# A fused attention and SwiGLU kernel on one core: gamma loads moved behind the first k and v, two casts moved off VectorE, the turns of A's x interleaved with Z's columns, three later jobs changed

## The chip, the cores and the metric

The kernel runs on one core of one Trainium2 chip. The metric is device time in microseconds (us). Most executions agree within 0.3%, so an effect of a few tenths of a microsecond needs several timed runs. Only fast runs are compared.

Names: PE is the tensor engine, DVE is VectorE, ACT is ScalarE, POOL is GpSimd, SP is SyncE, the engine whose queue issues nearly all DMAs here. "Span" is the time from the first to the last instruction in the profile. The device time is longer than the span by about 2 us.

## The reference, cut to what matters

```python
# q, k, v: (8, 8, 576, 64) f32; d_model 512, d_ff 1536; 4608 tokens
kv  = einsum('bhsd,bhse->bhde', k, v)
out = einsum('bhsd,bhde->bhse', q, kv)
out = out / sqrt(mean(out*out, -1) + 1e-6) * g_norm
x   = out.transpose(0, 2, 1, 3).reshape(4608, 512)
xn  = x / sqrt(mean(x*x, -1) + 1e-6) * rms_g
g   = xn @ w_gate
y   = (g * sigmoid(g) * (xn @ w_val)) @ w_out      # (4608, 512) f32
```

## The kernel before

The kernel works in bf16. It has a prologue for batch 0 (0 to about 22 us), a middle part in which the FFN of batch 0 runs beside the attention of batch 1 (to about 62 us), and a loop in which the FFN of batch n hides the attention of batch n+1. The tokens of batch 0 are split in two halves, A and Z. Each half goes through the same chain: q columns, squares, sums, square root, scale, turn of x (a transposition), first FFN units. The first FFN units also need the first two blocks of w_gate and w_val, loaded as f32 and cast.

The loads at the start, in order of issue, are nearly all on SP's queue; only two v loads and the two small gamma loads are on ACT's:

```python
for j in (0, 1):
    load_kv(0, "k", nc.sync, slice(j, j + 1))
    load_kv(0, "v", nc.scalar, slice(j, j + 1))
SC.preload_act_table(ACT.Sqrt)
nc.scalar.dma_start(out=gam[0:NS, :], in_=moe_rms_g...)        # gamma, two small loads
nc.scalar.dma_start(out=gam[NS : NS + 1, :]..., in_=g_norm...)
load_q0(0, nc.sync)                                            # two DMAs
for j in (2, 3):
    load_kv(0, "k", nc.sync, slice(j, j + 1))
    load_kv(0, "v", nc.sync, slice(j, j + 1))
load_q0(1, nc.sync)                                            # two DMAs
for blk in range(2):
    for name in ("g", "v"):
        load_w(blk, name, nc.sync)                             # w_gate and w_val, blocks 0 and 1
```

Each DMA completes into one of eight semaphores that are taken in turn. An issue therefore waits until the DMA eight places earlier has landed. I call these the eight completion slots.

Near the end of the prologue, Z's square root and the casts of weight block 1:

```python
Z.head()
Z.root_by_table(lambda: round_w(1, "g", 2, DVE))   # the square root, on ACT
round_w(1, "g", 0, SC)                             # casts of w_gate block 1, ACT
round_w(1, "g", 3, SC)
round_w(1, "g", 1, GP)
xs = [Z.scale(c, oZ[c]) for c in range(2)]
...
```

In the loop, the normalised rows of the next batch are turned by DMA, four times, on SP's queue, and the next FFN waits for the fourth:

```python
def x_rows(self, c):
    ...
    nc.sync.dma_start_transpose(
        out=xnts[self.n][:, :, 128 * c : 128 * c + 128],
        in_=self.xna[c].rearrange("p h d -> p (h d)"),
    )
```

## Time and profile before

| | before |
|---|---|
| time, median of the first three runs | 324.34 us (324.08 to 324.5) |
| profiled run: time, span | 324.46, 322.7 us |
| PE busy | 316.0 us, 98% |
| PE waits listed | four groups, 2.3 us together, all before 21.6 us |
| second half of q of batch 0: last byte landed | 12.88 us |
| v of batch 1: last byte landed | 37.11 us |
| first down-projection matmul | 41.31 us |

All waits of PE of more than 0.15 us (engine, tile and line, what it waited for, total us, times, longest):

```profile
PE att_ps L617 <- DVE sel L606: 1.2, 1, 1.2
PE att_ps L640 <- DVE qb L108: 0.5, 2, 0.3
PE v_ps L489 <- DVE wv_sb L203: 0.4, 1, 0.4
PE g_ps L403 <- ACT qt L106: 0.2, 1, 0.2
```

Stretches of the kernel before (window, its length, busy us of PE, PEld, DVE, ACT and POOL, PE clock, DMA share, and last the GB/s that DMA moved):

```profile
10.00:12.00 2.00, 1.87 (x35) 0.85 (x28) 1.48 (x7) 0.99 (x3) 0.00 (x0) 1.00 1.03 331
12.00:14.00 2.00, 1.75 (x26) 1.11 (x25) 0.94 (x5) 0.38 (x1) 0.86 (x1) 1.00 1.09 362
```

### The profile page before, as it was taken

How to read it: one execution, taken by the hardware profiler on the slowest of the kernel's cores; microseconds unless marked ns; L12 is line 12 of the kernel's file. 1: busy time of each engine (PE TensorE's matmuls, PEld its weight loads, DVE VectorE, ACT ScalarE, POOL GpSimd, SP SyncE). 2: the span in 40 equal slices, each digit the busy share in tenths (PEclk: the TensorE clock that was granted, in tenths of full speed). 3: DMA queues.
4: the chain of work that ended last, by engine and by line, in shares of the span. 5: the costliest groups of instructions: out<-in, count | busy, mean ns of one | idle time of the engine just before them, and what ended most of it. 6: DMA issues, size and time to landing. Idle time of an engine off the chain costs nothing.

```text
span 322.7 us, 5143 instructions
## 1 busy us (share of the span) xinstructions
PE 316.0 (98%) x1925; PEld 156.5 (49%) x1925; DVE 181.5 (56%) x373; ACT 178.3 (55%) x318; POOL 20.3 (6%) x42
## 2 busy tenths in 40 slices
PE   8899999999999999999999999999999999999995
PEld 3575456554455445544554454445544444444443
DVE  4785767568438922793279417850696068703310
ACT  3576447666757475747664766576554355223321
POOL 1363251100000000000000000000000000000000
PEclk9999999999999999999999999999999999999999
DMA  7999999887379557924792378936102600240014
GB/s 277 355 351 386 377 374 293 214 265 176 65 195 295 132 143 163 328 54 114 187 328 56 73 202 222 315 55 169 43 2 49 182 31 1 48 147 4 0 35 98
DMA packets 74421, 54.87 MB, mean 170 GB/s; under 512 B 42264, under 2 KB 67100, under 8 KB 74396
## 3 DMA queue, kind: packets, MB, share of 16 engines
q1 hardware_dynamic: 74016, 53.88, 58.4%
q10 hardware_dynamic: 380, 0.66, 0.6%
q8 instruction: 15, 0.25, 0.3%
q14 instruction: 10, 0.08, 0.1%
HBM read 37.75 MB, written 9.44 MB: 146 GB/s over the span
## 4 chain that ended last, share of the span: by engine, by line
PE 92%; DMA 4%; DVE 2%; SPq 0%; ACT 0%; issue 0%; DVEq 0%
PE g_ps L472 28%; PE v_ps L472 28%; PE o_ps L516 27%; DMA st<-in_q_dram 3%; PE att_ps L272 2%; PE att_ps L343 2%; PE v_ps L516 1%; PE g_ps L516 1%; DVE xna L453 1%; DMA out_dram<-o_sb 1%; PE v_ps L489 1%; PE o_ps L489 1%; PE g_ps L489 0%; PE att_ps L338 0%; PE att_ps L285 0%; PE att_ps L265 0%
## 5 line engine op out<-in xcount | busy, mean ns | idle before, releaser
L478 DVE TENSOR_TENSOR h_sb<-silu,v_ps 128x512 bf16<-128x512 bf16 x104 | 71.0, 683 | 110.3 <-ACT silu L477 66.9
L472 PE MATMUL g_ps<-xnt,wg_sb 128*128 128x512 bf16 x416 | 106.8, 379 | 0.0
L472 PE MATMUL v_ps<-xnt,wv_sb 128*128 128x512 bf16 x416 | 106.7, 379 | 0.0
L477 ACT ACTIVATE silu<-g_ps 128x512 bf16<-128x512 f32 x104 | 62.5, 601 | 64.4 <-PE g_ps L472 53.7
L516 PE MATMUL o_ps<-wo_sb,h_sb 128*128 128x512 bf16 x396 | 87.4, 379 | 0.0
L472 PEld LDWEIGHTS <-wv_sb 128*128 128x128 bf16 x416 | 40.7, 98 | 49.1
L516 PEld LDWEIGHTS <-h_sb 128*128 128x128 bf16 x420 | 40.7, 98 | 47.7
L472 PEld LDWEIGHTS <-wg_sb 128*128 128x128 bf16 x416 | 38.7, 98 | 40.0 <-issue 0.4
L106 ACT COPY o_sb<-o_ps 128x512 f32<-128x512 f32 (+1 forms) x34 | 19.7, 580 | 38.0 <-PE o_ps L516 37.3
L361 DVE TENSOR_REDUCE ssq<-sq 128x16 f32<-128x1024 bf16 x28 | 34.1, 1219 | 1.0
L352 ACT ACTIVATE sq<-att_ps 128x512 bf16<-128x512 f32 x28 | 16.7, 597 | 13.1 <-PE att_ps L343 8.7
L106 ACT CAST vb<-st 128x512 bf16<-128x512 f32 (+2 forms) x33 | 18.9, 625 | 4.7 <-DMA st<-in_v_dram 4.7
L378 DVE TENSOR_TENSOR xna<-outa,s1y 128x512 bf16<-128x512 bf16 x28 | 17.9, 684 | 0.0
L354 ACT CAST outa<-att_ps 128x512 bf16<-128x512 f32 x28 | 16.2, 579 | 0.0
L106 ACT CAST qb<-st 128x1024 bf16<-128x1024 f32 (+1 forms) x15 | 14.2, 987 | 1.9 <-DMA st<-in_q_dram 1.9
L106 ACT CAST kb<-st 128x512 bf16<-128x512 f32 (+1 forms) x25 | 14.0, 619 | 0.0
L360 DVE TENSOR_TENSOR sq<-sq,gsq 128x512 bf16<-128x512 bf16 x28 | 11.7, 418 | 0.0
L343 PEld LDWEIGHTS <-qt 128*128 128x128 bf16 x96 | 7.4, 98 | 5.7
L343 PE MATMUL att_ps<-kv_all,qt 128*128 128x128 bf16 x96 | 9.3, 219 | 0.0
L272 PEld LDWEIGHTS <-kb 128*128 128x128 bf16 x120 | 7.7, 98 | 2.8
L617 PE MATMUL att_ps<-kv_all 128*128 128x512 bf16 (+1 forms) x21 | 7.6, 490 | 1.2 <-DVE sel L606 1.2
L272 PE MATMUL att_ps<-vb,kb 128*128 128x128 bf16 x120 | 8.7, 219 | 0.0
(141 smaller groups left out, 166.9 us busy)
## 6 DMA issues: line engine op xcount, KB each, us to landing
st<-in_q_dram SPq DMA_DIRECT2D x7, 1024.0 KB, 6.5
out_dram<-o_sb SPq DMA_DIRECT2D x14, 512.0 KB, 3.2
st<-in_k_dram SPq DMA_DIRECT2D x6, 1024.0 KB, 10.2
st<-in_v_dram SPq DMA_DIRECT2D x6, 1024.0 KB, 11.2
st<-in_moe_w_out_dram SPq DMA_DIRECT2D x6, 512.0 KB, 11.4
st<-in_moe_w_gate_dram SPq DMA_DIRECT2D x4, 512.0 KB, 9.4
st<-in_moe_w_val_dram SPq DMA_DIRECT2D x4, 512.0 KB, 9.8
st<-in_k_dram SPq DMA_DIRECT2D x4, 288.0 KB, 4.0
```

The costliest lines, as they stand in the source:

```text
L106: engine.copy(out=dst, in_=src)
L272: PE.matmul(ps, lhsT=bufs[b]["k"][:, t, hs, :], rhs=bufs[b]["v"][:, t, hs, :], start=(first and t == 0), stop=(last and t == T),)
L343: PE.matmul(cols, lhsT=self.qt[:, j, 128 * c : 128 * c + 128], rhs=kv_all[:, self.n, j, :], start=(j == 0), stop=(j == NS - 1),)
L352: SC.activation(out=self.sq[c][:, 0], in_=ps, func=ACT.Square)
L354: SC.copy(out=self.outa[c], in_=ps)
L360: DVE.tensor_tensor(out=sq[:, 1], in0=sq[:, 0], in1=gsq8, op=OP.mult)
L361: DVE.reduce_sum(out=self.ssq[:, c], in_=sq, axis=AX.X)
L378: DVE.tensor_tensor(out=self.xna[c], in0=self.outa[c], in1=self.alpha[:, c, :].to_broadcast([128, H, D]), op=OP.mult)
L472: PE.matmul(ps, lhsT=wt[:, s, j * 128 : (j + 1) * 128], rhs=x[:, s, :], start=(s == 0), stop=(s == NS - 1),)
L477: SC.activation(out=silu, in_=g_ps, func=ACT.Silu)
L478: DVE.tensor_tensor(out=self.h[:, j, :], in0=silu, in1=v_ps, op=OP.mult)
L516: PE.matmul(self.o_ps[c], lhsT=self.h[:, j, c * 128 : (c + 1) * 128], rhs=wo_sb[:, j, :], start=(j == 0), stop=(j == NF - 1),)
```

## The change

Its intent is to start the dense part of PE earlier, the part in which PE runs one matmul after another. Gamma is needed late, so its loads go behind the first k and v and stop taking early completion slots there. Two casts move off DVE, which stands in A's and Z's chains. The turns of A's x are interleaved with Z's columns, so that A's first FFN units start earlier. Cleaning of the tail rows moves from GpSimd in the prologue to DVE beside dense FFN units. The diff, cut to its core:

```diff
     def load_q(b):
-        nc.sync.dma_start(out=..., in_=q[b, :, ...])
+        for hs in (slice(0, 4), slice(4, 8)) if b < EARLY else (slice(0, H),):
+            nc.sync.dma_start(out=...[:, hs], in_=q[b, hs, ...])
 ...
     SC.preload_act_table(ACT.Sqrt)
-    nc.scalar.dma_start(out=gam[0:NS, :], ...)
-    nc.scalar.dma_start(out=gam[NS : NS + 1, :]..., ...)
     load_q0(0, nc.sync)
     for j in (2, 3):
         load_kv(0, "k", nc.sync, slice(j, j + 1))
         load_kv(0, "v", nc.sync, slice(j, j + 1))
+    nc.sync.dma_start(out=gam[0:NS, :], ...)
+    nc.sync.dma_start(out=gam[NS : NS + 1, :]..., ...)
     load_q0(1, nc.sync)
 ...                                   # gamma's transposition on PE moves behind k, v number 3
-    cast_q0(1, hs0, DVE)
+    cast_q0(1, hs0, SC)
     cast_q0(1, hs1, GP)
     A.head()
+    A.root_by_table(lambda: None)
 ...
-    for j in range(NS):
-        columns(Z, j, banksZ[j // 2])
-    squares(Z, 0, banksZ[0])
-    squares(Z, 1, banksZ[1])
+    for i in range(2):
+        for j in (2 * i, 2 * i + 1):
+            columns(Z, j, banksZ[i])
+        squares(Z, i, banksZ[i])
+        x_turn(A, i, xs[i], DVE, ...)
 ...
-    Z.head()
-    Z.root_by_table(lambda: round_w(1, "g", 2, DVE))
     round_w(1, "g", 0, SC)
     round_w(1, "g", 3, SC)
     round_w(1, "g", 1, GP)
+    Z.head()
+    Z.root_by_table(lambda: round_w(1, "g", 2, DVE))
     xs = [Z.scale(c, oZ[c]) for c in range(2)]
-    for s, engine in enumerate((GP, SC, DVE, DVE)):
+    for s, engine in enumerate((GP, SC, GP, DVE)):
         round_w(1, "v", s, engine)
-    clear_tail_rows(0, GP)
 ...
+        if j == 7:
+            clear_tail_rows(0, DVE)
 ...
-    for i, engine in enumerate((DVE, SC, DVE, GP)):
+    for i, engine in enumerate((DVE, SC, DVE, SC)):
         cast_q(1, slice(2 * i, 2 * i + 2), engine)
```

I split it in three: the *gamma move* (loads and transposition), the *new order* of the prologue, and the *late parts* (q of batch 1 in two loads, tail memsets on DVE at unit 7, last q cast of batch 1 on ACT).

More of the change, by code (lines that the diff above doesn't have):

```diff
@@ L158, in load_q @@
         raws[b, "q"] = st
-        nc.sync.dma_start(
-            out=st.rearrange("p (h x) -> p h x", h=H),
-            in_=q[b, :, 0:MAIN, :].rearrange("h (p t) d -> p h (t d)", t=T),
-        )
+        for hs in (slice(0, 4), slice(4, 8)) if b < EARLY else (slice(0, H),):
+            nc.sync.dma_start(
+                out=st.rearrange("p (h x) -> p h x", h=H)[:, hs],
+                in_=q[b, hs, 0:MAIN, :].rearrange("h (p t) d -> p h (t d)", t=T),
+            )
     def alloc_q(b):
@@ L492, in half_unit, with up_pair @@
                 )
-        def up_pair(self, i, lo, between=(), banks=None):
+        def up_pair(self, i, lo, banks=None):
             banks = banks or self.pair_banks()
@@ L499, in up_pair @@
                     self.half_unit(banks[k], u, wt, 2 * i + u, lo, lo + 256)
-                    for f in between[2 * k + u :][:1]:
-                        f()
             return banks
@@ L587 @@
     SC.preload_act_table(ACT.Sqrt)
-    nc.scalar.dma_start(out=gam[0:NS, :], in_=moe_rms_g.rearrange("(s p) -> s p", p=128))
-    nc.scalar.dma_start(
-        out=gam[NS : NS + 1, :].rearrange("o (i d) -> o i d", i=2),
-        in_=g_norm.rearrange("(o d) -> o d", o=1).unsqueeze(1).to_broadcast([1, 2, D]),
-    )
     load_q0(0, nc.sync)
@@ L596 @@
         load_kv(0, "v", nc.sync, slice(j, j + 1))
+    nc.sync.dma_start(out=gam[0:NS, :], in_=moe_rms_g.rearrange("(s p) -> s p", p=128))
+    nc.sync.dma_start(
+        out=gam[NS : NS + 1, :].rearrange("o (i d) -> o i d", i=2),
+        in_=g_norm.rearrange("(o d) -> o d", o=1).unsqueeze(1).to_broadcast([1, 2, D]),
+    )
     load_q0(1, nc.sync)
@@ L670, in squares, with x_turn @@
         )
-    def x_turn(cols, c, x, engine, dummies=0):
-        bank = att_pool.tile([128, MAIN], FP32, name="att_ps")
-        warm(bank, dummies)
+    def x_turn(cols, c, x, engine, p=att_pool, name="att_ps"):
+        bank = p.tile([128, MAIN], FP32, name=name)
         to_rows(x, cols.n, cols.lo // 128 + c, bank.bitcast(BF16)[:, 0:512].rearrange("p (j t) -> p j t", j=NS), engine)
@@ L705 @@
     put_q0(0, qps, 1, SC)
+    kv2 = state0(2, 3)
+    cast_kv(0, "k", 3, DVE)
+    put_state0(2, kv2)
+    cast_kv(0, "v", 3, DVE)
     gam_ps = ops_pool.tile([128, 512], FP32, name="o_ps")
@@ L709 @@
     DVE.tensor_scalar(out=rowscale, in0=gam_ps[:, 0:NS], scalar1=gcol[:, 0:1], scalar2=None, op0=OP.mult)
-    kv2 = state0(2, 3)
-    cast_kv(0, "k", 3, DVE)
-    put_state0(2, kv2)
-    cast_kv(0, "v", 3, DVE)
     columns(A, 0, banksA[0])
@@ L732 @@
     oA = rows_of(A)
-    cast_q0(1, hs0, DVE)
+    cast_q0(1, hs0, SC)
     cast_q0(1, hs1, GP)
     A.head()
+    A.root_by_table(lambda: None)
     banksZ = [gps_pool.tile([128, MAIN], FP32, name="g_ps"), vps_pool.tile([128, MAIN], FP32, name="v_ps")]
-    qps = turn_q0(1, 0)
-    A.root_by_table(lambda: None)
+    qps = turn_q0(1, 2)
+    warm(banksZ[0], 2)
     for g in range(2):
         put_q0(1, qps, g, SC)
-    for name in ("g", "v"):
-        for s in range(NS):
-            if name == "g" or s < 2:
-                round_w(0, name, s, GP)
-    warm(banksZ[0], 2)
-    for j in range(NS):
-        columns(Z, j, banksZ[j // 2])
-    squares(Z, 0, banksZ[0])
-    squares(Z, 1, banksZ[1])
+    for s in range(NS):
+        round_w(0, "g", s, GP)
+    for s in range(2):
+        round_w(0, "v", s, GP)
+    xs = [A.scale(c, oA[c]) for c in range(2)]
+    for i in range(2):
+        for j in (2 * i, 2 * i + 1):
+            columns(Z, j, banksZ[i])
+        squares(Z, i, banksZ[i])
+        x_turn(A, i, xs[i], DVE, *((ops_pool, "o_ps") if i else ()))
     for s in (2, 3):
         round_w(0, "v", s, SC)
-    xs = [A.scale(c, oA[c]) for c in range(2)]
-    x_turn(A, 0, xs[0], DVE)
-    x_turn(A, 1, xs[1], DVE)
     ffn = Ffn(0)
@@ L762 @@
             Z.sums()
-    oZ = rows_of(Z)
     for u in range(2):
         ffn.half_unit(first[1], u, wv_sb, u, 0, 256)
-    Z.head()
-    Z.root_by_table(lambda: round_w(1, "g", 2, DVE))
+    oZ = rows_of(Z)
     round_w(1, "g", 0, SC)
@@ L770 @@
     round_w(1, "g", 1, GP)
+    Z.head()
+    Z.root_by_table(lambda: round_w(1, "g", 2, DVE))
     xs = [Z.scale(c, oZ[c]) for c in range(2)]
-    for s, engine in enumerate((GP, SC, DVE, DVE)):
+    for s, engine in enumerate((GP, SC, GP, DVE)):
         round_w(1, "v", s, engine)
     SC.preload_act_table(ACT.Silu)
-    clear_tail_rows(0, GP)
-    def turnsZ():
-        x_turn(Z, 0, xs[0], DVE)
-        x_turn(Z, 1, xs[1], DVE)
-    second = ffn.up_pair(1, 0, (lambda: None, turnsZ))
+    second = ffn.pair_banks()
+    for u in range(2):
+        ffn.half_unit(second[0], u, wg_sb, 2 + u, 0, 256)
+    for u in range(2):
+        x_turn(Z, u, xs[u], DVE)
+    for u in range(2):
+        ffn.half_unit(second[1], u, wv_sb, 2 + u, 0, 256)
     ffn.gate_pair(0, 0, first)
```

## The prediction

> **What bounds the kernel.** The whole-span page says TensorE 98% busy, and the chain of waits is 92% PE: from 21.5 us to the end the chain is one matmul after another, with no PE idle time. The change touches only the start and the jobs beside the dense part, so it can win only what moves the moment at which PE becomes dense (21.50 us, the second half of the first w_val units).
>
> The chain of waits before that moment: DMA of the first q half, its issue slot, DMA of the second q half (landed 12.9), DVE cast 12.97-13.40, A's root chain on DVE/ACT 13.40-14.72, scale 14.81-16.11, turn, first FFN units, Z's sums and root 17.2-19.08, Z's scale 19.17-20.46, two w_val casts on DVE until 21.45. So: load, DVE, load, DVE. From 3 to 31 us the stretches table shows all 16 DMA engines busy (share about 1.0, 320 to 410 GB/s): landings there depend on bytes in front of them, not on issue.
>
> **What the change does.**
> 1. The eight completion slots of the DMA issues shift: third k and v no longer wait for the first ones (1.2 us earlier issue); gamma costs SP 0.55 + 0.71 us, second q is issued about 0.3 us later. The Trainium skill (DMA: Bandwidth & Descriptors, "Queues, rings and completion order") says descriptors are consumed in ring order on each engine; with full rings I expect every landing unchanged: q 12.9, w_gate block 0 14.5, block 1 18.2, w_val block 1 19.7. Gamma lands behind v, near 10.5-11; its PE turn stands before A's columns and may hold them 0 to 0.5 us.
> 2. DVE loses the 0.43 us q cast, so A's root chain can start when its sums end (12.8) instead of 13.31: A up to 0.5 us earlier, less what gamma costs. But the first FFN units still need the fourth GpSimd cast of w_gate block 0 (ends 16.38, from the 14.5 landing): the first units gain about 0.2 us at most.
> 3. Z's square root now stands on ACT behind two casts of w_gate block 1, which cannot start before that block lands (18.2; GpSimd waited for it until 18.26 before). Two casts took 0.89 us, so the root starts near 19.05, not 18.57; scale of Z ends near 20.95, not 20.46: minus 0.5.
> 4. One w_val cast fewer on DVE (two took 1.33 us) and no GpSimd memsets there: plus about 0.6. The copies of Z's turned x end near 22.25 against 22.37.
>
> Sum: A's gain stops at weight landings; the Z chain loses 0.5 and wins 0.6. PE becomes dense about 0.1 us earlier, between 0.6 earlier and 0.4 later.
> 5. The rest (memsets on DVE at 2 x 0.27 us, the split of batch 1's q load, its last cast on ACT) lies where PE never waits. It gives slack to the query turn at 44.8 us, no time.
>
> **Prediction.** 324.2 us, 8 in 10 within 323.5 to 324.8. Faster by over 2%: 0.01; within 2%: 0.985; slower: 0.005.
>
> **What shows each step.** Landings (waits of GpSimd, ACT and DVE on DMA) within 0.3 us of before; DVE's first reciprocal of A before 13.2; ACT's second square root after 18.9, preceded by an idle wait for w_gate block 1; last copy of Z's turned x near 22.2; PE without gaps afterwards; same PE busy time plus two or three dummy matmuls.
>
> **What would make it wrong.** Block 1's w_gate lands clearly earlier or later than 18.2 (then Z's root moves with it, and the total by as much); gamma lands after 11.5 and holds PE so long that A's chain is late; a load after 26 us (v of batch 2 landed at 59.25, just before its casts at 59.29) becomes the limit once PE runs earlier.

## More of the kernel before

The profile's page of the kernel before, cut: the span; PE's busy time; busy tenths of PE and of the DMA engines in 40 slices of 8.1 us; one of the two queues that carry instructions; shares of the chain of waits.

```profile
span 322.7 us, 5143 instructions
...
PE 316.0 (98%) x1925; PEld 156.5 (49%) x1925; DVE 181.5 (56%) x373; ACT 178.3 (55%) x318; POOL 20.3 (6%) x42
...
PE   8899999999999999999999999999999999999995
...
DMA  7999999887379557924792378936102600240014
...
q14 instruction: 10, 0.08, 0.1%
...
PE 92%; DMA 4%; DVE 2%; SPq 0%; ACT 0%; issue 0%; DVEq 0%
```

PE is full nearly everywhere. But the DMA row is at 9 from the second slice to the seventh: for the first 57 us the DMA engines are as full as PE is.

SP's timeline of the kernel before, around the second q half and the first weights (start us, duration us, what was issued):

```profile
6.72 1.27 SPq L582 DMA_DIRECT2D st<-in_q_dram  x2
8.03 0.60 SPq L193 DMA_DIRECT2D st<-in_moe_w_gate_dram  x1
8.68 0.51 SPq L193 DMA_DIRECT2D st<-in_moe_w_val_dram  x1
9.23 0.51 SPq L193 DMA_DIRECT2D st<-in_moe_w_gate_dram  x1
9.78 1.20 SPq L193 DMA_DIRECT2D st<-in_moe_w_val_dram  x1
```

SP's timeline of the kernel before, around the third and fourth turn of batch 2's x and the store after them:

```profile
85.33 2.52 SPq L385 DMA_TRANSPOSE xnt<-xna  x2
88.35 0.37 SPq L539 DMA_DIRECT2D out_dram<-o_sb  x1
```

Two turns take 2.52 us together, and PE does not wait for them: nothing in PE's waits names xnt. Between the end of the turns (87.85) and the store (88.35) SP stands still for half a microsecond.

## The result, and the profile after

The changed kernel took 325.06 us (median of six runs, 324.79 to 325.45) against 324.3 (six runs, 324.08 to 324.5). The ratio is 1.0026, with a 95% interval of 1.0013 to 1.0039. Ratios here are the mean time of one kernel's fast runs over that of the other's of the same rounds, so not quite the ratio of the medians that I quote. It is in the class that was predicted, the same within 2%, but outside the predicted range, on the slow side by 0.26 us.

The page of the changed kernel, the same lines:

```profile
span 323.0 us, 5146 instructions
...
PE 315.8 (98%) x1927; PEld 157.1 (49%) x1927; DVE 180.6 (56%) x373; ACT 179.3 (56%) x320; POOL 18.1 (6%) x40
...
PE 88%; DVE 5%; DMA 3%; SPq 2%; issue 1%; ACT 1%; DVEq 0%
```

The page hardly changes. PE's share of the chain of waits fell from 92% to 88%. The waits of PE in the changed kernel say why:

```profile
PE att_ps L616 <- DVE sel L605: 1.2, 1, 1.2
PE att_ps L266 <- ACT vb L106: 0.7, 1, 0.7
PE g_ps L473 <- DMA xnt<-xna: 0.5, 1, 0.5
PE att_ps L639 <- DVE qb L108: 0.4, 1, 0.4
PE g_ps L404 <- ACT qt L106: 0.2, 1, 0.2
PE att_ps L266 <- DVE vb L108: 0.2, 1, 0.2
```

Two new waits lie in the dense part. The last line of this view is at the kv products of batch 1, near 40 us, where PE waits 0.2 us for a cast of v (the 0.7 us for ACT's cast, at the same line of code, is in the prologue). At L473, the first FFN unit of batch 2 at 89 us, PE waits 0.5 us for a DMA turn of x.

I aligned the two traces on the matmuls of the same place in the program. The changed kernel's PE is *ahead* by 0.75 us at 22 us and still by 0.70 at 34 us, but at the first down-projection, behind the kv products of batch 1, only by 0.31 (41.00 against 41.31). It is ahead by 0.22 at 62 us, and *behind* by 0.32 us from 89 us to the end, with no further change. So the prologue's gain in this pair of profiles is lost in the part that I had called dense, nearly all of it at two places (near 40 and 89 us; 0.1 us more goes at 61.5 us, the kv products of batch 2), and a little is added outside the span: time minus span is 1.99 to 2.06 us in all six runs, and 1.74 to 1.85 in all 55 runs of the kernel before whose span is on record.

The stretches at 10 to 14 us in the changed kernel. The DMA engines move about 25 GB/s less on average:

```profile
10.00:12.00 2.00, 1.78 (x42) 1.17 (x41) 1.57 (x6) 1.44 (x4) 0.00 (x0) 1.00 0.99 305
12.00:14.00 2.00, 1.93 (x24) 1.14 (x24) 1.03 (x6) 1.09 (x3) 0.61 (x1) 1.00 1.04 339
```

SP's timeline of the changed kernel, around the second q half and the first weights:

```profile
5.77 0.32 SPq L591 DMA_DIRECT2D gam<-in_moe_rms_g_dram  x1
6.14 0.70 SPq L592 DMA_DIRECT2D gam<-in_g_norm_dram  x1
7.03 1.30 SPq L581 DMA_DIRECT2D st<-in_q_dram  x2
8.48 0.52 SPq L194 DMA_DIRECT2D st<-in_moe_w_gate_dram  x1
9.50 0.38 SPq L194 DMA_DIRECT2D st<-in_moe_w_val_dram  x1
10.25 0.37 SPq L194 DMA_DIRECT2D st<-in_moe_w_gate_dram  x1
11.02 0.78 SPq L194 DMA_DIRECT2D st<-in_moe_w_val_dram  x1
```

The second q half is issued 0.3 us later, as predicted. But the weights behind it are issued 0.45, 0.82, 1.02 and 1.24 us later. SP's waits for 6 to 12 us name the cause: eight places ahead of each of these weight loads there now stands a k or v load of batch 0. Ahead of the two loads of block 0 it had been q and gamma, which had landed sooner (7.44 and 6.72 us; the k and v land at 8.46 and 9.48).

```profile
SPq L194 <- DMA st<-in_v_dram: 0.9, 2, 0.5
SPq L194 <- DMA st<-in_k_dram: 0.4, 1, 0.4
```

SP's timeline of the changed kernel, around the third and fourth turn of batch 2's x:

```profile
85.08 2.92 SPq L386 DMA_TRANSPOSE xnt<-xna  x2
88.11 0.52 SPq L538 DMA_DIRECT2D out_dram<-o_sb  x1
```

The two turns take 2.92 us instead of 2.52. The half microsecond in which SP stands still is now *between* them, and the store follows at once. The next line is PE at that place; the bracket is the idle time before the group and what ended it.

```profile
89.54 0.81 PE L473 MATMUL g_ps<-xnt,wg_sb 128*128 128x512 bf16 x3 [0.48 <-DMA xnt<-xna]
```

Numbering SP's trace records (issues and semaphore waits) from zero, the pause of 0.45 us stands ahead of record 79 in *both* kernels. Before, record 79 is a store; after, it is the fourth turn, since SP has two records more ahead of it (two gamma loads and one q load more, one semaphore wait fewer). A second pause, of 0.37 us, stands ahead of record 207, which is 128 later, in both kernels.

### The profile page after: what moved, and what is told of

The parts are those of the page before. It is cut to its first block, busy times and chain, and to the rows that moved or that the text cites. A ratio compares the mean times of both kernels' runs of the same rounds, so it can differ in the third digit from the quotient of the medians.

```text
span 323.0 us, 5146 instructions
## 1 busy us (share of the span) xinstructions
PE 315.8 (98%) x1927; PEld 157.1 (49%) x1927; DVE 180.6 (56%) x373; ACT 179.3 (56%) x320; POOL 18.1 (6%) x40
## 4 chain that ended last, share of the span: by engine, by line
PE 88%; DVE 5%; DMA 3%; SPq 2%; issue 1%; ACT 1%; DVEq 0%
PE g_ps L473 27%; PE v_ps L473 26%; PE o_ps L515 23%; PE att_ps L273 2%; DMA st<-in_v_dram 2%; PE att_ps L344 2%; DVE h_sb L479 1%; PE v_ps L490 1%; DMA xnt<-xna 1%; PE v_ps L515 1%; PE g_ps L515 1%; DVE xna L379 1%; DMA out_dram<-o_sb 1%; SPq L386 1%; PE att_ps L266 1%
## 5 line engine op out<-in xcount | busy, mean ns | idle before, releaser
L473 PE MATMUL g_ps<-xnt,wg_sb 128*128 128x512 bf16 x416 | 106.8, 379 | 0.5 <-DMA xnt<-xna 0.5
L473 PE MATMUL v_ps<-xnt,wv_sb 128*128 128x512 bf16 x416 | 106.8, 379 | 0.0
L473 PEld LDWEIGHTS <-wv_sb 128*128 128x128 bf16 x416 | 40.6, 98 | 49.2 <-DVE wv_sb L204 0.5
L473 PEld LDWEIGHTS <-wg_sb 128*128 128x128 bf16 x416 | 38.7, 98 | 40.6 <-issue 0.9
L106 ACT CAST qb<-st 128x1024 bf16<-128x1024 f32 (+1 forms) x17 | 15.4, 944 | 2.0 <-DMA st<-in_q_dram 1.8
```

The source lines that it names most:

```text
L106: engine.copy(out=dst, in_=src)
L473: PE.matmul(ps, lhsT=wt[:, s, j * 128 : (j + 1) * 128], rhs=x[:, s, :], start=(s == 0), stop=(s == NS - 1),)
```

## The experiments

Theory P: SP stops for about 0.45 us at every 128th instruction, and the change moved such a stop into the turns of x. Theory S: gamma on SP takes two completion slots and about 1.1 us of SP, so weights are issued late and the DMA engines run short at 10 to 14 us. Rivals: the slower casts of v or the reordered casts are to blame (then undoing P or S would gain nothing), or chance between executions. The kernel before ran beside every set: medians 324.42, 324.38, 324.51, 324.58 and 324.53 us on five chips, 11 runs each.

### e1: the changed kernel again, unaltered

> The changed kernel, unaltered, for a second profile. Theory P (position): the sequencer of SP stops for about 0.45 us between two of its instructions wherever one of its blocks of 128 instructions ends; in both first profiles that was just ahead of the instruction with number 79 in SP's order, which in the changed kernel is the fourth turn by DMA of batch 2's x. Then the gap of 0.45 us ahead of that fourth turn and the PE wait of about 0.5 us near 89 us must be there again, and the time is 324.8 to 325.3. Rival R (chance): the gap is a hiccup of one execution; then it is gone or elsewhere in this profile. Also expected again: PE 0.7 us ahead of before at 24 us, and a PE wait for the v casts of batch 1 near 40 us.

It took 325.32 us, ratio 1.0024 (1.0009 to 1.0040), span 323.2. The pause stood between the third and fourth turn again, and PE waited 0.5 us for xnt again. The loss is real and does not belong to one execution.

### e2: the kernel before, with two instructions more on SP

```diff
     load_batch(2)
+    for _ in range(2):
+        nc.sync.drain()
```

> The kernel before with two empty SP instructions (drains[...]) after the prologue's loads, so that the fourth turn of batch 2's x takes the same place in SP's order as in the changed kernel. Theory P: a gap of about 0.45 us ahead of that turn, PE waits about 0.4 us near 89 us, the time is 0.3 to 0.5 us above before. Rival R: same time as before within 0.1 us and no gap there.

SP's timeline and PE's in this run:

```profile
84.60 2.92 SPq L385 DMA_TRANSPOSE xnt<-xna  x2
```

```profile
89.04 1.02 PE L472 MATMUL g_ps<-xnt,wg_sb 128*128 128x512 bf16 x4 [0.46 <-DMA xnt<-xna]
```

Two drains, instructions that do no work here (0.4 us together at 53.2 us, in a stretch of 2 us in which SP waits anyway) put the pause between the turns and make PE wait. So the place in SP's program is enough to make the wait, without anything else of the change. The time was 324.54 us, ratio 1.0003 (0.9986 to 1.0020), where 0.3 to 0.5 us above the kernel before had been expected: the cost itself is not told from noise by this run's times.

### e3: the changed kernel, with seven instructions more on SP

```diff
     load_batch(2)
+    for _ in range(7):
+        nc.sync.drain()
```

> The changed kernel with seven empty SP instructions, so that the block of SP's instructions ends ahead of the long wait before the first turn of batch 2's x. Theory P: no gap between the turns, no PE wait near 89 us, and the time is 0.4 to 0.6 us below the changed kernel, 324.4 to 324.7. Rival R: same as the changed kernel within 0.1 us.

It took 324.84 us, ratio 1.0009 (0.9994 to 1.0023), so 0.48 below e1, as expected, though above the expected 324.4 to 324.7. SP's timeline, and then all of PE's waits:

```profile
69.28 3.20 SPq L137 DMA_DIRECT2D st<-in_v_dram  x1
82.82 1.24 SPq L386 DMA_TRANSPOSE xnt<-xna  x1
```

```profile
PE att_ps L616 <- DVE sel L605: 1.2, 1, 1.2
PE att_ps L639 <- DVE qb L108: 1.1, 1, 1.1
PE o_ps L709 <- DMA gam<-in_g_norm_dram: 0.6, 1, 0.6
PE att_ps L266 <- ACT vb L106: 0.4, 1, 0.4
PE g_ps L404 <- ACT qt L106: 0.2, 1, 0.2
```

The pause (0.46 us, ahead of record 79 again) now falls into the ten microseconds from 72.5 to 82.8 in which SP has nothing to issue, and the wait for xnt is gone.

### e4: the changed kernel, gamma's loads back on ACT's queue

```diff
-    nc.sync.dma_start(out=gam[0:NS, :], ...)
-    nc.sync.dma_start(out=gam[NS : NS + 1, :]..., ...)
+    nc.scalar.dma_start(out=gam[0:NS, :], ...)
+    nc.scalar.dma_start(out=gam[NS : NS + 1, :]..., ...)
```

> The changed kernel with the two gamma loads issued by ACT instead of SP, at the same place in the program. SP then has two instructions fewer, and the fourth turn of batch 2's x stands ahead of the end of the block, as in the kernel before. Theory P: no PE wait near 89 us, 0.4 to 0.6 us below the changed kernel. The second q and the weights are issued about 1.0 us earlier by SP, which by itself should move nothing, since the DMA engines are busy then. Rival R: no difference over 0.1 us.

ACT issues them at 1.70 us, as in the kernel before, so this undoes the gamma move; and SP loses the two instructions, so the pause is back ahead of the store. It took 324.27 us, ratio 0.9990 (0.9974 to 1.0006): 1.05 us below e1 and 0.57 below e3, which has the gamma move but not the badly placed pause. The weights were issued at 7.96, 8.62, 9.17 and 9.72 us, and the DMA engines moved 340 and 357 GB/s in the two stretches. That is twice the gain that I had expected. This looked like the whole loss found. It was not, as the repetitions (e10, e15) show.

### e5: the kernel before, with two small loads on SP that nobody reads

```diff
+    spare = consts.tile([8, 128], FP32, name="spare")
+    nc.sync.dma_start(out=spare[0:NS, :], in_=moe_rms_g...)
+    nc.sync.dma_start(out=spare[NS : NS + 1, :]..., in_=g_norm...)
     load_q0(1, nc.sync)
 ...
     load_batch(2)
+    for _ in range(5):
+        nc.sync.drain()
```

> The kernel before, its gamma loads left on ACT, with two more loads of the same 2.0 and 0.5 KB into a tile that nothing reads, issued by SP where the changed kernel issues gamma, and five empty SP instructions so that the end of SP's block does no harm. Theory S (slots): eight loads may be under way; two tiny ones behind the third and fourth k and v take two of the eight slots and 1.2 us of SP's issue, so the weights of block 0 and 1 are issued 0.8 to 1.2 us later, the DMA engines run short between 10 and 14 us (under 310 GB/s in 10 to 12 us, 331 to 352 without), v of batch 1 lands 0.4 to 0.8 us later, and the time is 0.3 to 0.6 us above before. Rival W (waiting for gamma): what the move cost was PE standing at gamma's turn, which nothing does here; then the time is that of before within 0.15 us.

It took 326.27 us, ratio 1.0054 (1.0034 to 1.0074), five fast runs. The sign and the late weight issues (10.88 us for w_gate block 1 against 9.23) agree with theory S, but the run does not isolate it. Five drains were too few: the trace shows the pause (0.46 us, ahead of record 79) between the first and the second turn of batch 2's x, so theory P may have taken its share here too. The size, 1.9 us against its own rounds (medians 326.27 and 324.38) where 0.3 to 0.6 was expected, is more than both theories give and is unexplained. The profiled execution was slow, 670 us with every matmul about twice as long, so its profile cannot be compared; I have no cause for it.

### e6 and e11: the kernel before, with the late parts only

```diff
+        for hs in (slice(0, 4), slice(4, 8)) if b < EARLY else (slice(0, H),):   # load_q in two
-    clear_tail_rows(0, GP)
+        if j == 7:
+            clear_tail_rows(0, DVE)
-    for i, engine in enumerate((DVE, SC, DVE, GP)):
+    for i, engine in enumerate((DVE, SC, DVE, SC)):
```

> The kernel before with only the late parts of the change: batch 1's q load in two halves, the tail memsets on DVE at unit 7, the last q cast on ACT instead of GpSimd. Expected: no change of the span over 0.15 us, since PE never waited there. Open: the time outside the span (time minus span) was 1.75 to 1.85 us in before and 1.99 to 2.06 in every kernel with the whole change; if this kernel shows 2.0, it comes with these parts (three GpSimd instructions fewer), if 1.8, with the reordered prologue.

> The kernel before with the late parts of the change only, again: 323.9 to 324.3 if its 323.98 was real, time minus span 2.0 to 2.06 again, the fastest of the four if the profiles are to be trusted.

323.98 us, ratio 0.9992 (0.9977 to 1.0007), and on another chip 324.31, ratio 0.9995 (0.9980 to 1.0009). Neither interval leaves 1. What is clear of noise is the time outside the span: it is 1.99 to 2.10 in all twelve runs, so it comes with the late parts. The span itself is shorter by some 0.4 us, where I had expected no change over 0.15.

### e7: the kernel before, with the new order only

The edit is the changed kernel with gamma back on ACT and the late parts undone; gamma's transposition stays late.

> The kernel before with only the reordered prologue (q cast on ACT, Z's columns between A's turns, later rows of Z, w_val casts moved); gamma and the late parts as before. Expected from the run with gamma on ACT (PE 0.9 us ahead of before at 24 us, 0.7 at the end): span 0.3 to 0.7 us below before, time 0.1 to 0.7 below, by whether the 0.2 us outside the span come with this part.

324.69 us, ratio 1.0007 (0.9991 to 1.0024): no gain from the part that was meant to bring it. Time minus span was 1.91 to 1.98, 0.15 above the kernel before.

### e8 and e9: the kernel before, with the gamma move only

```diff
-    nc.scalar.dma_start(out=gam[...], ...)     # twice
+    nc.sync.dma_start(out=gam[...], ...)       # twice, ahead of load_q0(1, nc.sync)
 ...                                            # transposition behind k, v number 3
     load_batch(2)
+    for _ in range(7):                         # e8 only
+        nc.sync.drain()
```

> Theory S (two gamma loads between the last k and v and the second half of q take two of the eight completion slots and about 1.2 us of SyncE, so the weight loads are issued later and the DMA engines run short at 10 to 14 us): the kernel before with the move of gamma alone (load and transposition), and seven drains that put the end of SyncE's instruction block into a stretch in which it waits anyway. Expect weight loads issued 0.7 to 1.2 us later than before, under 345 GB/s at 10 to 14 us on average, and 324.7 to 325.1 us against 324.4. Rival R (the loss in the changed kernel belongs to gamma together with the new order of the prologue): this run is within 0.2 us of before. Time minus span: 1.8 if what lies outside the span belongs to the reordering, 2.0 if to gamma.

> The same without the drains: SyncE has two instructions more ahead of the turns of batch 2, so theory P (a stop of about 0.45 us ahead of every 128th instruction of SyncE) puts the stop ahead of the fourth DMA turn of x: a PE wait of about 0.5 us on xnt at 89 us, and 0.3 to 0.5 us above e8. Without P: equal to e8.

e8 took 324.73 us, ratio 1.0011 (0.9992 to 1.0030); e9 took 325.08, ratio 1.0025 (1.0010 to 1.0041). So the gamma move alone, with the badly placed pause that it brings, is as slow as the whole change. e9's waits hold the line, and e8's do not:

```profile
PE g_ps L472 <- DMA xnt<-xna: 0.4, 1, 0.4
```

The stretches of e8, 307 GB/s on average where the kernel before has 347:

```profile
10.00:12.00 2.00, 0.92 (x22) 0.80 (x22) 1.38 (x6) 0.89 (x2) 0.00 (x0) 1.00 1.07 329
12.00:14.00 2.00, 1.93 (x34) 0.94 (x33) 1.10 (x6) 1.26 (x3) 0.30 (x1) 1.00 0.86 286
```

Time minus span is 1.8 in both, so what lies outside the span does not come from gamma.

### e10: e4 again

> The changed kernel with gamma alone back on ScalarE's queue, again, to see whether it beats the kernel before: if its 324.27 was real, 324.1 to 324.4 and a ratio of 0.998 to 1.000; an interval that holds 1 leaves it the same as before. Time minus span 2.0 again.

324.69 us, ratio 1.0015 (0.9996 to 1.0034). The gain of e4 did not repeat. The profile shows one way in which this kernel loses an execution. ACT's timeline in e10:

```profile
18.67 0.91 ACT L202 ACTIVATE wg_sb<-st,rowscale 128x256 bf16<-128x256 f32 x2 [1.34 <-DMA st<-in_moe_w_gate_dram]
19.48 0.20 ACT L447 ACTIVATE Zs<-Zz 128x16 f32<-128x16 f32 x1
```

Z's square root (Zs) stands behind two casts that wait for w_gate block 1, which landed at 18.65 here. In e12 below, with the old order, the block landed at 18.56, just as late, and the root was done first:

```profile
18.22 0.22 ACT L446 ACTIVATE Zs<-Zz 128x16 f32<-128x16 f32 x1 [1.28 <-DVE Zz L230]
18.58 0.91 ACT L201 ACTIVATE wg_sb<-st,rowscale 128x256 bf16<-128x256 f32 x2
```

In the seven profiles that have the new order unaltered (the changed kernel, e1, e3, e4, e7, e10, e15) the root starts 0.83 to 0.99 us after that landing, which itself scatters from 17.56 to 18.65 us.

### e12: the kernel before, with one instruction more on ACT

Which part of the late parts costs 0.2 us outside the span? By then, by my count of the compiled programs (not in the traces), all kernels with 483 or more compiled instructions on ACT had it and all with 482 or fewer had not.

```diff
                 step()
+    nc.scalar.drain()
```

> The kernel before with one drain at the end of ScalarE's program: 483 compiled instructions on ScalarE in place of 482, nothing else. Theory C (the time outside the span goes with the count of ScalarE's instructions): time minus span 2.0 in place of 1.8, span as before, time 324.6 to 324.7. Rival M (it goes with the work that was moved, the memsets or casts): 1.8, and the time of before.

Time minus span was 1.77 to 1.84: unchanged. 324.57 us, ratio 1.0001 (0.9987 to 1.0014). The count of ACT's instructions is not the cause.

### e13: the late parts without the ACT cast

The last q cast of batch 1 stays on GpSimd; else as e6.

> The kernel before with the late parts (q in two loads, tail memsets on VectorE at unit 7), but the last q cast left on GpSimd, so that ScalarE has 482 instructions as before. Theory C: time minus span 1.8, span 322.1 to 322.3 as in e6 and e11, time 323.9 to 324.1, a little faster than both kernels. Rival M: 2.0 outside the span.

324.77 us, ratio 1.0007 (0.9993 to 1.0020), and time minus span 2.14 to 2.18, the largest of all. So the theory falls and rival M stands as far as it goes: the time outside the span comes with the split of q or the moved memsets, or both. Which of them, and by what mechanism, stays open; no profile shows what happens outside the span. It also failed as a faster kernel.

### e14 and e15: Z's root ahead of the two casts, and the same kernel without that

```diff
     oZ = rows_of(Z)
+    Z.head()
+    Z.root_by_table(lambda: round_w(1, "g", 2, DVE))
     round_w(1, "g", 0, SC)
     round_w(1, "g", 3, SC)
     round_w(1, "g", 1, GP)
-    Z.head()
-    Z.root_by_table(lambda: round_w(1, "g", 2, DVE))
```

> The changed kernel with gamma back on ScalarE's queue and Z's square root ahead of the two w_gate casts. Theory Z (the new order costs about 0.25 us on average because the root waits for a landing that scatters): root at 18.0 to 18.6 whatever the landing, 0.15 to 0.35 us below e15 on average, and 323.9 to 324.2. Rival (the cost of the new order lies elsewhere, or is chance): equal to e15 within 0.1 us.

> The changed kernel with gamma on ScalarE's queue, as e4 and e10 (324.27 and 324.69): 324.3 to 324.7, root 0.8 to 1.0 us after w_gate block 1 lands.

e14 took 324.61 us, ratio 1.0001 (0.9988 to 1.0014), not the 323.9 to 324.2 that I had expected, and its root started at 18.66, just outside the expected 18.0 to 18.6; e15 took 324.82, ratio 1.0016 (0.9996 to 1.0037). The means differ by 0.41 us, in the direction expected, but without one run of e15 at 326.34 by only 0.14, so this agrees with theory Z and does not show it. No kernel beats the kernel before beyond noise.

### All profiles together

One profile per kernel, e5 left out. In us: when w_gate block 1 and the main part of v of batch 1 had landed (the record of the last of 16 engines), when the first down-projection matmul started, from that landing of v to this start, from this start to the end of the last matmul, and the mean of time minus span over the runs.

| profile | w_gate 1 | v of batch 1 | first down | down − v | end − down | outside |
|---|---|---|---|---|---|---|
| before | 18.18 | 37.11 | 41.31 | 4.21 | 277.5 | 1.8 |
| after | 17.57 | 37.26 | 41.00 | 3.74 | **278.2** | 2.0 |
| e1 after again | 18.01 | 37.27 | 41.03 | 3.76 | **278.4** | 2.0 |
| e2 before, two drains | 17.98 | 36.88 | 40.61 | 3.72 | **278.1** | 1.8 |
| e3 after, seven drains | 18.43 | 37.32 | 41.45 | 4.13 | 277.5 | 2.0 |
| e4 gamma undone | 17.56 | 36.47 | 40.47 | 4.00 | 277.6 | 2.0 |
| e6 late parts | 17.87 | 36.76 | 40.48 | 3.72 | 277.5 | 2.0 |
| e7 new order | 18.16 | 36.99 | 41.38 | 4.39 | 277.5 | 1.95 |
| e8 gamma move, pause elsewhere | 18.15 | 37.62 | 41.75 | 4.13 | 277.5 | 1.8 |
| e9 gamma move | 17.71 | 36.67 | 40.85 | 4.18 | **278.0** | 1.8 |
| e10 as e4 | 18.65 | 37.57 | 41.50 | 3.93 | 277.5 | 2.05 |
| e11 as e6 | 17.51 | 36.57 | 40.36 | 3.79 | 277.5 | 2.0 |
| e12 one drain on ACT | 18.56 | 37.47 | 41.21 | 3.74 | 277.5 | 1.8 |
| e13 late parts, cast on GpSimd | 17.92 | 37.55 | 41.70 | 4.15 | 277.5 | 2.2 |
| e14 as e4, root first | 18.11 | 37.03 | 40.79 | 3.76 | 277.5 | 2.0 |
| e15 as e4 | 18.42 | 37.33 | 41.27 | 3.94 | 277.5 | 2.0 |

Four things can be read here.

- From the first down-projection on, a kernel takes 277.5 us, or 278.0 to 278.4. The second kind are the four whose pause falls between the turns of x. That is theory P with hardly any noise in it. The differences are 0.4 to 0.9 us; compared matmul by matmul with the kernel before, each of the four loses 0.51 to 0.55 us at the one place near 89 us, and the changed kernel and e1 lose a further 0.1 and 0.3 near 61.5 us, at the kv products of batch 2.
- The first down-projection is never less than 3.72 us after v of batch 1 has landed, and in seven of sixteen profiles it is within 0.07 us of that. In these seven, v's landing sets the time, or nearly. In the other nine it starts 0.2 to 0.7 us later than that after v: there it is PE that comes late out of the prologue. Where PE is early, as in the changed kernel, it waits at the kv products of batch 1.
- When v lands scatters by 1.15 us between executions, also between executions of the same program (e4 and e10: 36.47 and 37.57). That is as large as any effect in question. One pair of profiles can therefore not say what the prologue gained or lost.
- PE's own arrival scatters as much. Its first FFN matmuls of 512 columns started at 26.14, 25.25 and 25.81 us in the three profiles with the prologue of the kernel before (before, e2, e12), and at 25.39, 25.73 and 26.19 in the three with that of the changed kernel (after, e1, e3). The means are 25.73 and 25.77. So the 0.75 us "ahead" is a difference of two executions, and no gain of the new prologue is shown.

To size the parts from times I fitted 148 fast runs of before, after and e1 to e15 (without e5; of the first set, the first three runs of the kernel before) as a sum: one level for each of the six sets of runs, plus one term for each part that a kernel has. The new order with the root first (e14) has a term of its own, +0.04 (0.23). Standard errors are in brackets. This assumes that the parts add up.

| part | time, us | span alone, us |
|---|---|---|
| gamma move, without the pause | +0.34 (0.13) | +0.36 (0.13) |
| pause between the turns of x | +0.33 (0.13) | +0.31 (0.13) |
| new order of the prologue | +0.32 (0.12) | +0.29 (0.12) |
| late parts | −0.07 (0.10) | −0.30 (0.10) |
| sum | +0.92 | +0.66 |

The changed kernel's mean lay 0.83 us above the kernel before in e1's rounds, so the sum accounts for it. The rival of the reordered casts is thus not excluded: the new order as a whole costs as much as either theory's part.

## Why the prediction was wrong

The prediction had the whole change at 0.1 us of gain. Two of its steps failed in their mechanism: step 1 (the landings) and step 5 (the late jobs). The fit gives +0.34 us for the gamma move of step 1 and +0.33 for the pause that step 5 overlooked; the pause is shown by its own experiments, the way of the other to the end is not. The new order of steps 2 to 4 costs a further +0.32, and its cause stays open.

**What bounds the kernel: half right.** PE is 98% busy and the time after the first down-projection is PE's alone. But "from 21.5 us to the end the chain is one matmul after another" described one execution in which PE happened to arrive at the kv products of batch 1 just as v had been cast. The table shows that arriving earlier is worth no more than v of batch 1 allows: in the pair, v landed at 37.11 and 37.26 us, and of PE's lead of 0.70 us only 0.31 was left behind the kv products.

**Step 1 failed: "with full rings I expect every landing unchanged".** The Trainium skill (DMA: Bandwidth & Descriptors, "Queues, rings and completion order") says that an engine works through its descriptors in ring order; nothing here contradicts it, and no run here tests it alone. My inference from it was wrong: it left out that SP's issues must keep the rings full. The gamma loads used two of the eight slots and 1.1 us of SP (5.77 to 6.84), so the last of the four weight loads went out 0.98 us later (mean of the five profiles with gamma on SP, 10.95 us, against 9.97 in the eleven others). The second q half landed at 13.25 us on average against 12.70, w_gate block 0 at 14.93 against 14.33. At 10 to 14 us DMA moved 318 GB/s on average in the five (306 to 334) against 341 in the eleven (313 to 359); 23 GB/s for 4 us are 92 KB, which at 341 GB/s is 0.27 us. That estimate, from those rates, is of the size of the fitted cost of the gamma move, 0.34 (0.13), which does not prove that the one makes the other. I had costed SP's issue time, and had not followed what the shifted slots make the *later* issues wait for. What stays open is by which way the cost reaches the end: the later landings do not show it, w_gate block 1 (17.98 against 18.08) and v of batch 1 (37.23 against 37.07) differing by less than they scatter. In the one pair of before and after, q came 0.30 us later, which is within the 0.3 that I had allowed; block 1, 0.61 us earlier, was not.

**Gamma's own turn on PE: right.** "May hold PE 0 to 0.5 us": 0 in the changed kernel's profile, 0.3 to 0.7 in e1, e3, e8 and e9, so the upper end was a little low.

**Step 2: too hopeful.** A's first reciprocal started at 13.40, not before 13.2; it had been 13.31. The q cast no longer stood in front of it, but DVE now waited 0.8 us for A's sums from PE, whose first columns had started at 10.79 instead of 10.09, so A gained nothing. Over the two times three profiles with these prologues it started at 13.72 on average, against 13.05.

**Step 3: the mechanism was right; the pair of profiles hid it by accident.** The root does stand behind two casts that wait for w_gate block 1, so it follows that landing by 0.8 to 1.0 us. In the profile after, the block landed at 17.57 instead of 18.18 and the root came at 18.55, as before; in e10 it came at 19.48. Over the two times three profiles it came at 18.94 on average, against 18.28: 0.66 later, where I had 0.48. I had named this dependence as what would make the prediction wrong. This dependence is a candidate for the new order's +0.32 (0.12); e14 agrees with that without showing it.

**Step 4 and the sum: better than predicted in the pair, not in the mean.** The last copy of Z's turned x ended at 21.43 against 22.37, where I had 22.25. PE was ahead by 0.75 us instead of 0.1. Over the two times three profiles the copy ended at 21.81 against 21.96, and PE's arrival was the same within 0.05 us, so a lead of 0.75 us is not shown for the new prologue. In the pair, the kv products of batch 1 then took 0.4 of it, behind casts of a v that landed at 37.26.

**Step 5 failed: "lies where PE never waits".** I looked for work that moved and found none on PE's path. What moved was SP's place in its own program. Two instructions more put a pause of 0.45 us into the one stretch of SP in which PE waits for the fourth turn. The kernel before had the pause just behind that turn, by luck. This is 0.33 (0.13) us of the times, and a wait of 0.44 to 0.48 us in each of the four profiles. And the late parts, which I had at no time at all, cost 0.2 us outside the span, cause open, and seem to save 0.3 inside it.

**A cause that is argued, not shown:** the pause looks like the fetch of SP's next instructions. It comes at records 79 and 207, so 128 apart; the instruction queue q14 brings packets of 8192 bytes, which is 128 instructions at 64 bytes; and where e3 moved the two pauses (to 72.9 and 257.5 us, from 86.8 and 282.5 in the changed kernel), two of these packets moved with them (to 76.9 and 259.1, from 87.7 and 283.2). But the packets start 0.6 to 4.0 us after the pause has ended, so the pause is not the wait for the packet that follows it. The Trainium skill (Runtime: NRT & Kernel Launch, "Instruction fetch mechanics") gives 16 KiB blocks of 256 instructions, which is where the 64 bytes are from, and says of crossing a block's end that the cost is mostly hidden. The other instruction queue, q8, does bring packets of 16384 bytes. For SP the measurement differs: pauses 128 records apart, of 0.45 and 0.37 us.

## What to carry to other kernels

When a change adds or removes instructions on an engine that issues DMAs, list that engine's pauses in the trace, and look what they fall on before and after; a tight run of DMAs that PE waits for is best kept clear of them, and two empty instructions were enough here to shift a pause. A small load on a full queue costs its issue time and its completion slot, so follow the slots of the loads *behind* it, not only its own. And before reading a gain from one profile, see how far the landings scatter between executions of one and the same program: here 1.1 us, more than any part that the fit found.

## What the Trainium skill lacked or had wrong

- Runtime: NRT & Kernel Launch, "Instruction fetch mechanics", gives refills in 16 KiB blocks and a mostly hidden cost. SP paused 0.45 and 0.37 us ahead of records 79 and 207, 128 apart, and q14 moved 8192-byte packets (q8 did move 16384); that the pause is a refill is not shown. The first pause cost PE 0.4 to 0.5 us where a DMA turn stood behind it.
- Runtime: NRT & Kernel Launch, "The launch sequence", gives one duration for each stage that surrounds a kernel, and a total that depends on engine count and DMA setup. Here time minus span went from 1.8 us to 1.95, 2.0 or 2.17 us between kernels with the same inputs and the same outputs, steadily for each kernel. I found nothing more on that page that tells what in a kernel changes it.
- DMA: Bandwidth & Descriptors, "Queues, rings and completion order", describes rings. That a queue can run short because the kernel's own completion semaphores are taken in turn, eight in this kernel, I did not find there; with two small loads moved to SP, DMA moved 318 GB/s on average at 10 to 14 us (five profiles), against 341 in eleven others.
- No page that I read gives the scatter of landings between executions of one kernel: v of batch 1 landed at 36.47 and 37.57 us in two executions of the same program.
